# Windowed attention and a two-layer network on one core: a new written order of all steps, first-layer sums in any order of head pairs, copies on other engines, more DMA transposes, no warming matmuls

## The chip, the core and the metric

The kernel runs on one core of a Trainium2 chip. The metric is the device time of one execution in microseconds (us). A profiled execution has a span too, from its first to its last instruction; the span is what the views of the profile divide up, and it is a little shorter than the time.

## The reference

Eight batches of eight heads of width 64 attend; each batch has 512 local and 32 global tokens. What comes out, 544 tokens a batch and 512 wide, goes through two dense layers with a hard swish between them.

```python
k_all = concatenate([k_g, k_l]);  v_all = concatenate([v_g, v_l])
out_g = softmax(q_g @ k_all.T / 8) @ v_all                 # 32 global queries see all 544 keys
s_ll  = where(abs(i - j) <= 32, q_l @ k_l.T / 8, -1e9)     # 512 local queries: a band of local keys
s_lg  = q_l @ k_g.T / 8                                    # ... and the 32 global keys
out_l = softmax(concatenate([s_lg, s_ll])) @ concatenate([v_g, v_l])
x     = concatenate([out_g, out_l])                        # as (8 * 544, 512): heads side by side
h     = x @ w_in                                           # 512 -> 2048
out   = (h * clip(h + 3, 0, 6) / 6) @ w_out                # 2048 -> 512
```

Inputs and output are float32; the kernel multiplies in float16 and sums in float32.

## The kernel before

**Units of work.** The attention part goes by head pair: pair p (0 to 31) is two heads of batch p // 4, put side by side so that they fill the 128 partitions. The dense part goes by batch f (0 to 7) for the local tokens and once more (f = 8) for the 256 global tokens of all batches. The first layer makes 16 blocks c of 128 hidden rows by 512 tokens, each a sum of four matmuls, one for each head pair m of the batch (`w_in` is kept as four tiles by m). The second layer makes four quarters t of 128 tokens by 512 outputs, each a sum of sixteen matmuls over c.

**A list of tokens.** Nothing is in a loop. The whole program is one list of words, `ORDER` (L514 on), 2069 of them, which `run(ORDER.split())` (L688) takes one after the other; each word names a small helper and its arguments. `pin(*ALL)` (L689) then ties the instructions of every engine, and those of the SP queue that starts the transfers, into the order in which they were written. So an engine does its instructions in the order of the list, and each waits where its operands or its output buffer are not ready. A second string, `SEATS`, gives for each tile in turn the number of the buffer that it takes: seven PSUM banks `ps0` to `ps6` (the eighth holds the global output), 13 staging buffers for loads, three or four for most others.

**The words**, by helper (an engine letter at the end of a word is v for VectorE, g for GpSimd, a for ScalarE):

- `ld`, `lw`, `lg`, `lv`: load one pair's q, k or v (256 KB of float32 to a staging tile), a piece of the weights, the global q and k, the global v. All but `lv` (GpSimd's queue) go by the SP queue.
- `ca`, `cw`, `Gc`: cast what was loaded to float16 (`copy`, L133). `vs`, `vg`, `vG`, `kg`, `qw`: shift or copy pieces of v, of the global v and k, and the wrap of 32 columns of q. `fv`, `fg`, `fe`, `fk`, `ov`, `qz`, `iv`, `ig`, `im`, `ik`: fills of constants and masks.
- `Tp` and `Te`: transpose q or k on TensorE (four 128-wide matmuls) and copy it out of PSUM; or `Td` (L243): the same by a DMA transpose, one instruction of the SP queue. `Gp`, `Ge` do it for the global q and k.
- `Sp` (L286): scores of a pair for one of two windows of keys (ch 0 and 1), eight matmuls over 64 rows into two banks. `Se` (L296): exponential of one bank on ScalarE. `Sv` (L300): product with the 0/1 mask on VectorE. Where `Sm` ran first (two 512-wide matmuls adding -30000 outside the band), there is no `Sv`.
- `Ap` (L333, L336) and `An` (L345, L346): attention times values, and division by the sum of the exponentials, on VectorE. `Qp`, `Qe`, `Pp`, `Ga`, `Gv`: the same for the global queries.
- `Xp` and `Xe`, or `Xd` (L372): transpose the normalised result into the activations `xt` of the dense part, on TensorE with a copy, or by a DMA transpose.
- `Hp` (L408): matmuls m0 to m1 of first-layer block c of batch f. `Ha` (L413): relu of (h + 3) / 6 on ScalarE. `Hv` (L419): min with 1 and times h on VectorE, which frees the PSUM bank. `Op` (L426): four of the sixteen matmuls of a quarter t. `Oe`: copy it out. `Os` (L442): store it.
- `wm` (L495): warming matmuls, 512 wide on zeros, whose result nothing reads.

**How the order is staged.** The list opens with batch 0's loads, casts and scores, with the weights' loads among them; from then on the dense part of batch f is written between the attention steps of batch f + 1, and the loads for later batches with them. The last stretch has only dense work. The two lines that fix the order of a first-layer sum before are in `H_pe`: the bank is taken when `m0 == 0`, and the sum starts at m == 0 and stops at m == 3; so pair 0 is first and pair 3 last. `O_pe` is written in the same way over c.

The functions that the diff touches:

Of the kernel before, what the change touches and what calls it, by code (L numbers as in the profile page):

```python
# [14 lines left out]
def kernel(  # L15
# [40 lines left out]
ps 01234560123455401054036254631405623160243524341624132540134236503651631653106451034561204513240513015320465  # L56
10465461530421350623061350464301354063406342630456230452543025362350652436056504132653640306431463142301645341
20463213256016243056410263425130130512215321504260621365031640351202635410345265436513246164024325251206130541
52651341056201456104352614306241356525041236012453561031204215463245632456016061346521340264035640256010623416
5 ;  # L60
stg 0123456789abc0145362798b0a1c53647289a0b1c356489a27b103c645892a7b103c6589247bac03592681ba47053268cb17403529
a61cb748309c6b75831a65b4a3c ;
kn 01320132013201320132031013210323 ;
qn 01230123012301203132132302130213 ;
qT 01230213021302130203210230130202 ;
E 01210210210212012010210210201021 ;
xn 01201201201202102101201210210210 ;
t1 01230120120320321032103210321032103210321032103120312013023102310231213201320132013213023120312031201231023
1030132103123012312121302130213013012 ;
ot 0123023230120230301101303132132013  # L70
# [327 lines left out]
    gts = {}  # L398

# [3 lines left out]
    def H_pe(f, c, m0, m1):  # L403
        if m0 == 0:
            st["H", f, c] = ps_tile("psH")
        for m in range(m0, m1):
            x = xg[:, m].rearrange("p b s -> p (b s)") if f == B else xts[f, m]
            nc.tensor.matmul(out=st["H", f, c][:, 0:FN(f)], lhsT=w_in_t[m][:, c * P:(c + 1) * P],  # L408
                             rhs=x, start=(m == 0), stop=(m == NM - 1), skip_group_check=True)
# [12 lines left out]
    def O_pe(f, t, c4):  # L422
        if c4 == 0:
            st["O", f, t] = ps_tile("po")
        for c in range(4 * c4, 4 * c4 + 4):
            nc.tensor.matmul(out=st["O", f, t][:, 0:dm], lhsT=gts[f, c][:, t * P:(t + 1) * P],  # L426
                             rhs=w_out_t[c // 4][:, c % 4], start=(c == 0), stop=(c == NC - 1))
# [87 lines left out]
id ld.1.q iv wm.7 ld.1.k fg.1.v ld.0.q fv.0.v ld.2.q lg.k.0 fv.1.v ld.0.k ca.1.q.g ld.3.k lv.0 Tp.1.q ov.1.0  # L515
ld.2.k ca.1.k.g Te.1.q.a ld.3.q ig ov.0.0 Tp.1.k qw.1.v ld.0.v ov.0.1 lw.i.7 im Gc.k.0.g ov.0.2 ld.1.v
Te.1.k.v Gp.k.0 ov.0.3 ca.0.k.g lw.i.4 Ge.k.0.v ca.2.q.g lw.i.12 Tp.0.k Te.0.k.v lw.i.0 Tp.2.q Sm.1.0 Te.2.q.a
ca.3.k.v Sm.0.0 vg.0.2.v ca.0.q.a vg.0.1.v Sm.1.1 ca.2.k.g lw.i.3 kg.0.v Tp.0.q vg.0.0.v fk.0 Te.0.q.a Sp.1.1
ld.2.v Sp.1.0 Se.1.1.1 qw.0.v Sp.0.0 Se.1.0.1 Sp.0.1 ca.0.v.g ld.3.v Se.0.0.0 wm.4 vs.0.g ca.3.q.a lw.i.1
Se.0.1.0 qw.2.g Tp.3.k Tp.2.k Se.0.1.1 Sm.2.0 Te.2.k.v ca.1.v.g lw.i.5 Se.1.1.0 ik vs.1.g Se.1.0.0 Sp.2.0  # L520
lw.i.2 Sm.2.1 Se.0.0.1 vg.0.3.g Sv.0.1.0 lw.i.8 Sv.0.1.1 Sp.2.1 Se.2.0.0 cw.i.12.g Tp.3.q cw.i.7.v Se.2.0.1
Ap.0.1 lw.i.6 cw.i.0.g Te.3.q.v Ap.0.0 Se.2.1.1 Ap.1.0 lw.i.13 cw.i.4.g qw.3.v Te.3.k.a Ap.1.1 An.1.0 Sm.3.0
Se.2.1.0 An.0.0 Sm.3.1 ca.2.v.g lw.i.10 fe.0 An.1.1 Sp.3.0 vs.2.g Sp.3.1 An.0.1 Se.3.0.0 Xp.1 ca.3.v.g lw.i.9
Se.3.0.1 Xp.0 Ap.2.0 Xe.0.v vs.3.g Ap.2.1 Se.3.1.1 lw.o.0 An.2.0 Hp.0.7.0.1 Se.3.1.0 cw.i.1.g Hp.0.1.0.1
lw.i.11 An.2.1 Hp.0.3.0.1 Xe.1.a Ap.3.1 Ap.3.0 cw.i.3.a cw.i.2.g ld.4.q An.3.1 Hp.0.1.1.2 Xp.2 qz Hp.0.5.0.1
cw.i.5.v lw.i.14 Hp.0.3.1.2 An.3.0 Hp.0.2.0.2 cw.i.6.g lw.o.1 Hp.0.7.1.2 Xe.2.a Xp.3 Hp.0.5.1.2 ov.1.1 Xe.3.v
Hp.0.2.2.3 Hp.0.7.2.3 fe.1 fe.3 cw.i.8.v lw.i.15 Hp.0.7.3.4 Hp.0.1.2.4 Ha.0.7 lw.o.7 Hp.0.10.0.1 Hp.0.4.0.1
Ha.0.1 Hp.0.4.1.2 Hv.0.7 Hp.0.5.2.3 cw.i.9.g lw.o.2 Hp.0.4.2.3 ov.1.2 Hp.0.4.3.4 Hv.0.1 cw.i.10.g Hp.0.2.3.4
ld.4.k cw.i.13.a Hp.0.5.3.4 Hp.0.0.0.1 cw.o.0.g Hp.0.0.1.2 Ha.0.2 lg.k.1 Hp.0.0.2.3 cw.i.11.g Hp.0.0.3.4
Ha.0.5 Hp.0.3.2.3 Hv.0.2 Hp.0.11.0.2 Ha.0.4 Hp.0.11.2.3 fe.2 Hp.0.10.1.2 cw.i.14.g Hp.0.10.2.3 Ha.0.0 Hv.0.4  # L530
Hp.0.10.3.4 Hp.0.11.3.4 ca.4.q.g Hp.0.9.0.1 Ha.0.10 lw.o.3 Hv.0.0 Hp.0.9.1.3 cw.o.1.g ov.1.3 Hp.0.9.3.4
cw.i.15.v lg.q.0 Tp.4.q Hp.0.14.0.1 Ha.0.9 Hv.0.10 Hp.0.14.1.3 Ha.0.11 Hp.0.14.3.4 Hv.0.9 Hp.0.12.0.2
Hp.0.3.3.4 Hv.0.5 Hp.0.12.2.4 Ha.0.3 ca.4.k.g Hp.0.13.0.1 Te.4.q.v Hp.0.13.1.2 Ha.0.14 Hp.0.13.2.3 lw.o.5
Hv.0.3 Hp.0.13.3.4 Hp.0.6.0.1 Ha.0.12 Gc.k.1.g lw.o.6 Hp.0.6.1.2 Hv.0.14 Hp.0.6.2.3 Ha.0.13 lw.o.4 Gp.k.1
cw.o.3.g Hv.0.12 Hp.0.6.3.4 Hp.0.8.0.1 ld.5.q cw.o.2.g Hp.0.8.1.2 Ha.0.6 Ge.k.1.v Hp.0.8.2.3 Hv.0.13
Hp.0.8.3.4 ld.5.k Hp.0.15.0.1 Tp.4.k lw.o.8 kg.1.v Op.0.1.0 Te.4.k.a fk.1 cw.o.7.v lw.o.11 Ha.0.8 Hv.0.11
cw.o.5.g Op.0.2.0 lw.o.10 qw.4.v Hv.0.6 cw.o.6.g lw.o.9 Sp.4.1 Gc.q.0.g lw.o.13 Hv.0.8 Hp.0.15.1.2 Se.4.1.0
Hp.0.15.2.4 lw.o.12 Se.4.1.1 Gp.q.0 Op.0.0.0 ca.5.q.g lw.o.15 cw.o.4.a Sv.4.1.1 Ha.0.15 Ge.q.0.v Op.0.0.1
lw.o.14 Hv.0.15 cw.o.8.g ld.6.q Sp.4.0 ca.5.k.g Qp.0 cw.o.11.v ld.4.v Se.4.0.1 Qp.3 Op.0.1.1 Sv.4.1.0 lv.1
Se.4.0.0 ld.6.k Qe.3 Tp.5.k fg.0.g Sv.4.0.0 Qp.1 ld.5.v Op.0.2.1 cw.o.10.v cw.o.9.a Te.5.k.a ld.7.q Op.0.1.2  # L540
vG.0.g Qe.0 cw.o.12.v ld.8.k cw.o.13.g Tp.5.q Qe.1 Sv.4.0.1 Op.0.0.2 ld.7.k cw.o.15.g Te.5.q.a Pp.0 cw.o.14.v
ld.6.v Pp.1 qw.5.v Op.0.0.3 ca.6.q.v ld.7.v Tp.6.q Op.0.1.3 Oe.0.0.a ca.4.v.g ld.8.q Te.6.q.a Sp.5.1 Oe.0.1.a
vs.4.v Sp.5.0 vg.1.0.g vg.1.3.v Op.0.2.2 Se.5.1.0 vg.1.2.v vg.1.1.v qw.6.g Se.5.0.0 ca.6.k.v ld.10.q Ap.4.1
Se.5.0.1 Ap.4.0 Tp.6.k Se.5.1.1 Op.0.2.3 An.4.0 ca.5.v.g ld.9.q Te.6.k.a An.4.1 Qp.2 Sv.5.1.0 ld.9.k Sp.6.0
Qe.2 Sp.6.1 vs.5.v Oe.0.2.v Op.0.3.0 Se.6.0.0 ca.7.q.v Se.6.1.0 ld.11.v Xp.4 Sv.5.0.0 Tp.7.q Se.6.1.1 Qp.6
Sv.6.1.0 Qp.4 ca.7.k.g Xe.4.a Op.0.3.1 Sv.6.1.1 Se.6.0.1 Sv.5.1.1 Op.0.3.2 Sv.5.0.1 Te.7.q.a Sv.6.0.1 Qe.4
# [135 lines left out]
Hp.8.13.1.3 Op.8.1.0 Op.8.1.1 Hp.8.8.3.4 Op.7.2.3 Ha.8.8 Hv.8.8 Hp.8.13.3.4 Hp.8.12.3.4 Op.7.3.1 Oe.7.2.a  # L682
Ha.8.13 Os.7.2 Op.8.1.2 Ha.8.12 Hv.8.13 Hv.8.12 Op.7.3.2 Op.8.1.3 Op.7.3.3 Oe.8.1.v Op.8.0.0 Os.8.1 Oe.7.3.a
Oe.7.1.a Op.8.0.1 Op.7.0.0 Os.7.3 Op.8.0.2 Os.7.1 Op.8.0.3 Op.7.0.1 Oe.8.0.a Op.7.0.2 Os.8.0 Op.7.0.3 Oe.7.0.a
Os.7.0
"""

    run(ORDER.split())  # L688
# [31 lines left out]
```

## Time and profile before

| what | value |
|---|---|
| runs of the kernel | 322.07, 318.54, 321.63 us (median 321.63) |
| span of the profiled execution | 318.3 us, 7431 instructions |
| mean granted TensorE clock | 0.991 |
| TensorE busy | 306.1 us (96%), 2787 matmuls |
| VectorE busy | 222.1 us (70%), 538 instructions |
| ScalarE busy | 217.6 us (68%), 434 |
| GpSimd busy | 86.8 us (27%), 155 |
| DMA | 53.06 MB, mean 167 GB/s |

The engines run side by side, so the shares don't add up to one. Matmuls are pipelined, and their busy time says that one was in the array, not how densely they follow each other; the spacing of their starts says that. Busy GpSimd lies in the first half above all (five to seven tenths of each of the first six slices of a fortieth of the span, nothing in the last nine). The profiled execution's own time is its span and what lies around it; the runs in the table are timed without the profiler, and the span is 0.2 us below the lowest of them.

### The profile page before, as it was taken

The numbers are of one execution on the slowest core, as the hardware profiler recorded it, in microseconds if no ns is written. First come the engines' busy times: TensorE is split into PE (matmuls) and PEld (weight loads), VectorE is DVE, ScalarE is ACT, GpSimd is POOL, SyncE is SP. The second block draws the span as 40 slices with busy tenths as digits, with TensorE's granted clock in tenths as the row PEclk, the third lists the DMA queues.
The fourth block names the chain that finished last, engine by engine and source line by source line (L and its number), as shares of the span: only waits on it lengthen the run. The fifth ranks groups of instructions, "written<-read, shape, count | busy, mean of one in ns | idle before, by whom it ended". The sixth has DMA issues, their size and how long they took to land.

```text
span 318.3 us, 7431 instructions
## 1 busy us (share of the span) xinstructions
PE 306.1 (96%) x2787; PEld 161.6 (51%) x2787; DVE 222.1 (70%) x538; ACT 217.6 (68%) x434; POOL 86.8 (27%) x155
## 2 busy tenths in 40 slices
PE   5889999999999999999998999999999999999994
PEld 1554455754555554554553546445555546456541
DVE  6496986979998996688753885589638667486120
ACT  5589787889656866878666986586748853477031
POOL 5766574723310223151103812412003000000000
PEclk9799999999999999999999999999999999999998
DMA  7999999598899988999999995694541004400033
GB/s 220 300 260 365 249 355 268 113 178 170 201 173 215 234 185 176 206 190 184 193 237 202 242 224 105 140 208 94 142 107 59 2 16 101 148 3 0 0 97 104
DMA packets 140293, 53.06 MB, mean 167 GB/s; under 512 B 127712, under 2 KB 131808, under 8 KB 140256
## 3 DMA queue, kind: packets, MB, share of 16 engines
q1 hardware_dynamic: 138080, 52.32, 71.8%
q0 software_dynamic: 2176, 0.26, 1.3%
q8 instruction: 22, 0.36, 0.5%
q14 instruction: 15, 0.12, 0.1%
HBM read 35.13 MB, written 8.91 MB: 138 GB/s over the span
## 4 chain that ended last, share of the span: by engine, by line
PE 84%; DVE 8%; DMA 3%; ACT 1%; issue 1%; SPq 1%; POOL 1%; DVEq 0%
PE psH L408 35%; PE po L426 34%; PE psS L286 5%; PE pav L333 2%; PE pav L336 2%; DVE E L300 2%; PE pg L360 2%; DMA xt<-xn 2%; DMA stg<-in_k_g_dram 1%; DVE xn L346 1%; PE psSG L310 1%; ACT E L296 1%; PE psS L274 1%; DVE gt L419 1%; PE psTq L248 1%
## 5 line engine op out<-in xcount | busy, mean ns | idle before, releaser
L426 PE MATMUL po<-wout,gt 128*128 128x512 f16 x544 | 131.7, 379 | 0.1
L408 PE MATMUL psH<-xt,win 128*128 128x512 f16 x512 | 125.2, 379 | 1.4 <-DMA xt<-xn 1.2
L419 DVE SCALAR_TENSOR_TENSOR gt<-t,psH 128x512 f16<-128x512 f32 (+1 forms) x144 | 89.0, 652 | 37.3 <-ACT t L413 36.2
L413 ACT ACTIVATE t<-psH,half_col 128x512 f32<-128x512 f32 (+1 forms) x144 | 89.6, 666 | 32.7 <-PE psH L408 27.7
L296 ACT ACTIVATE E<-psS 128x512 f16<-128x512 f32 x128 | 68.9, 609 | 26.0 <-PE psS L286 22.0
L408 PEld LDWEIGHTS <-win 128*128 128x128 f16 x576 | 53.0, 98 | 53.3 <-issue 1.8
L426 PEld LDWEIGHTS <-gt 128*128 128x128 f16 x544 | 49.2, 97 | 50.5 <-issue 0.4
L300 DVE TENSOR_TENSOR E<-E,mk 128x512 f16<-128x512 f16 x112 | 49.2, 469 | 15.3 <-ACT E L296 14.9
L346 DVE TENSOR_TENSOR xn<-pav,rc 128x256 f16<-128x256 f32 x64 | 27.2, 424 | 2.2
L133 ACT COPY ot<-po 128x512 f32<-128x512 f32 x23 | 13.3, 589 | 21.7 <-PE po L426 18.4
L333 PE MATMUL pav<-vt,E 128*128 128x65 f16 x256 | 22.9, 193 | 0.6 <-DVE qT L133 0.3
L336 PE MATMUL pav<-vb,E 128*128 128x65 f16 x256 | 22.9, 193 | 0.2
L333 PEld LDWEIGHTS <-E 128*128 128x128 f16 x256 | 18.9, 97 | 5.0 <-DVE E L300 0.5
L286 PEld LDWEIGHTS <-kT 64*128 64x128 f16 x512 | 14.6, 94 | 13.3 <-issue 11.1
L286 PE MATMUL psS<-qT,kT 64*128 64x128 f16 x512 | 21.0, 217 | 0.3 <-DVE qT L133 0.3
L345 DVE RECIPROCAL rc<-pav 128x4 f32<-128x4 f32 x64 | 11.2, 175 | 13.3 <-PE pav L336 13.1
L336 PEld LDWEIGHTS <-E 128*128 128x128 f16 x256 | 17.6, 97 | 4.8 <-issue 0.4
L133 POOL CAST qn<-stg 128x512 f16<-128x512 f32 x20 | 13.0, 651 | 24.7 <-DMA stg<-in_q_l_dram 24.4
L133 POOL CAST vt<-stg 128x512 f16<-128x512 f32 x20 | 12.9, 643 | 24.9 <-DMA stg<-in_v_l_dram 20.1
L133 POOL COPY vb<-vt 64x512 f16<-64x512 f16 x20 | 12.7, 640 | 23.0 <-DVE vt L133 17.6
L133 POOL CAST kn<-stg 128x512 f16<-128x512 f32 x15 | 10.4, 694 | 27.5 <-DMA stg<-in_k_l_dram 25.1
L314 ACT ACTIVATE Eg<-psSG 128x256 f16<-128x256 f32 x32 | 12.6, 392 | 5.3 <-PE psSG L310 3.3
(89 smaller groups left out, 248.3 us busy)
## 6 DMA issues: line engine op xcount, KB each, us to landing
stg<-in_q_l_dram SPq DMA_DIRECT2D x32, 256.0 KB, 4.0
stg<-in_k_l_dram SPq DMA_DIRECT2D x32, 256.0 KB, 3.9
stg<-in_v_l_dram SPq DMA_DIRECT2D x32, 256.0 KB, 3.9
out_dram<-ot SPq DMA_DIRECT2D x24, 256.0 KB, 3.2
stg<-in_moe_w_in_dram SPq DMA_DIRECT2D x16, 256.0 KB, 5.8
stg<-in_moe_w_out_dram SPq DMA_DIRECT2D x16, 256.0 KB, 5.1
out_dram<-ot SPq DMA_DIRECT2D x8, 192.0 KB, 2.7
out_dram<-ot SPq DMA_DIRECT2D x16, 64.0 KB, 1.9
```

The lines of the kernel that those rows point to most:

```text
L133: (nc.scalar.copy if eng == "a" else ENG[eng].tensor_copy)(out=out, in_=in_)
L286: nc.tensor.matmul(out=st[p, ch][e][:, w * P:(w + 1) * P], lhsT=kT[r, c0:c0 + P], rhs=qT[r, w * P:(w + 1) * P], start=not added, stop=True ...
L296: nc.scalar.activation(out=E_of(p)[:, ch, e], in_=st[p, ch][e], func=EXP, scale=qk_scale)
L300: nc.vector.tensor_tensor(out=E[:, ch, e], in0=E[:, ch, e], in1=mk[:, ch].rearrange("p w c -> p (w c)"), op=mult)
L314: nc.scalar.activation(out=Eg[:, 0:NT].rearrange("p u e s -> p (u e s)"), in_=ps[:, 0:NT * 2 * Sg], func=EXP, scale=qk_scale)
L333: nc.tensor.matmul(out=o, lhsT=E[:, 0, e, w * P:(w + 1) * P], rhs=vt[:, w, h, 0:D + 1], start=True, stop=False, skip_group_check=True)
L336: nc.tensor.matmul(out=o, lhsT=E[:, 1, e, w * P:(w + 1) * P], rhs=vb[:, (w - 1) % NT, h, 0:D + 1], start=False, stop=True, skip_group_chec ...
L346: nc.vector.tensor_tensor(out=st[p, "xn"][:, 2 * w2:2 * w2 + 2].rearrange("p w (e d) -> p w e d", e=2), in0=pv[:, :, :, 0:D], in1=rc.to_br ...
L408: nc.tensor.matmul(out=st["H", f, c][:, 0:FN(f)], lhsT=w_in_t[m][:, c * P:(c + 1) * P], rhs=x, start=(m == 0), stop=(m == NM - 1), skip_gr ...
L413: nc.scalar.activation(out=t1[:, 0:FN(f)], in_=st["H", f, c][:, 0:FN(f)], func=RELU, bias=half_col, scale=1.0 / 6.0)
L419: nc.vector.scalar_tensor_tensor(out=gts[f, c][:, 0:n], in0=st["t", f, c][:, 0:n], scalar=1.0, in1=st["H", f, c][:, 0:n], op0=amin, op1=mult)
L426: nc.tensor.matmul(out=st["O", f, t][:, 0:dm], lhsT=gts[f, c][:, t * P:(t + 1) * P], rhs=w_out_t[c // 4][:, c % 4], start=(c == 0), stop=( ...
```

## The change

`ORDER` and `SEATS` are replaced as a whole (2162 words for 2069), and two helpers are changed so that the terms of a sum may be written in any order:

```diff
+    added = {}
...
     def H_pe(f, c, m0, m1):
-        if m0 == 0:
+        if ("H", f, c) not in st:
             st["H", f, c] = ps_tile("psH")
         for m in range(m0, m1):
+            k = added["H", f, c] = added.get(("H", f, c), 0) + 1
             x = xg[:, m].rearrange("p b s -> p (b s)") if f == B else xts[f, m]
             nc.tensor.matmul(out=st["H", f, c][:, 0:FN(f)], lhsT=w_in_t[m][:, c * P:(c + 1) * P],
-                             rhs=x, start=(m == 0), stop=(m == NM - 1), skip_group_check=True)
+                             rhs=x, start=(k == 1), stop=(k == NM), skip_group_check=True)
...
     def O_pe(f, t, c4):
-        if c4 == 0:
+        if ("O", f, t) not in st:
             st["O", f, t] = ps_tile("po")
         for c in range(4 * c4, 4 * c4 + 4):
+            k = added["O", f, t] = added.get(("O", f, t), 0) + 1
             nc.tensor.matmul(out=st["O", f, t][:, 0:dm], lhsT=gts[f, c][:, t * P:(t + 1) * P],
-                             rhs=w_out_t[c // 4][:, c % 4], start=(c == 0), stop=(c == NC - 1))
+                             rhs=w_out_t[c // 4][:, c % 4], start=(k == 1), stop=(k == NC))
...
     ORDER = """
-id ld.1.q iv wm.7 ld.1.k fg.1.v ld.0.q fv.0.v ld.2.q lg.k.0 fv.1.v ld.0.k ca.1.q.g ld.3.k lv.0 Tp.1.q ov.1.0
-ld.2.k ca.1.k.g Te.1.q.a ld.3.q ig ov.0.0 Tp.1.k qw.1.v ld.0.v ov.0.1 lw.i.7 im Gc.k.0.g ov.0.2 ld.1.v
...
+fk.0 lg.k.0 lv.0 iv ov.0.0 ov.0.1 ov.1.0 ld.3.k id ig Gc.k.0.g fv.1.v ov.0.2 qz ov.1.1 im ld.1.k fv.0.v vg.0.1.v
+ov.0.3 ca.1.k.a ld.1.q ld.3.q ca.1.q.a ca.3.q.v Sm.1.1 ca.3.k.v Gp.k.0 Ge.k.0.v Tp.1.q Te.1.q.a qw.1.v Tp.1.k Tp.3.q
...
```

What the new list holds, word against word:

| words | before | after |
|---|---|---|
| `wm` (warming) | 2 words, 11 matmuls | none |
| `Sm` / `Sv` (mask by matmul / by product) | 8 / 112 | 7 / 114 |
| `Td`, `Xd` (DMA transposes of k and of activations) | 22, 23 | 24, 25 |
| `Tp` of k, `Xp` (the same on TensorE) | 10, 9 | 8, 7 |
| `ca` of k, q, v on GpSimd | 15, 20, 20 | 4, 3, 8 |
| ... on VectorE | 9, 8, 8 | 19, 21, 8 |
| ... on ScalarE | 8, 4, 4 | 9, 8, 16 |
| `vs` on GpSimd / VectorE / ScalarE | 20 / 12 / 0 | 4 / 15 / 13 |
| `vg` on GpSimd / VectorE / ScalarE | 12 / 16 / 4 | 9 / 18 / 5 |
| `qw` on GpSimd / VectorE | 18 / 14 | 5 / 27 |
| `Oe` (copy out of the second layer) on ScalarE / VectorE | 23 / 11 | 15 / 19 |
| `Hp` | 478 words, 576 matmuls | 576 words, 576 matmuls |

The `Hp` words now name one matmul each, and a block may begin with any pair. The first loads on the SP queue are those of k_g, then k of pairs 3 and 1 and q of pairs 1 and 3; before they were q and k of pair 1, q of 0 and 2, then k_g. Apart from the mask words, what is computed from what is the same.

## The prediction

> **What bounds the kernel now.** I read the page first (engine shares, clock, chain of waits), then the windows and the chain of the first 27 us, then the groups by line and shape for prices.
>
> ```profile
> PE 306.1 (96%) x2787; PEld 161.6 (51%) x2787; DVE 222.1 (70%) x538; ACT 217.6 (68%) x434; POOL 86.8 (27%) x155
> PEclk9799999999999999999999999999999999999998
> PE 84%; DVE 8%; DMA 3%; ACT 1%; issue 1%; SPq 1%; POOL 1%; DVEq 0%
> ```
>
> TensorE is busy 96% of the span, and the chain that ended last runs through it for 84%. A busy share hides how densely matmuls follow each other, so I price TensorE by spacing, from the chain and the timeline: 52 output matmuls take 11.24 us (0.216 each); a 256-wide one 0.109, a 128-wide transpose 0.056, an attention-value one 0.0295, a global score 0.029, a global value 0.025, a block of eight score matmuls 0.27.
>
> ```profile
> 2.79 4.47 DMA stg<-in_k_g_dram
> 7.31 0.60 POOL kgn L133
> ...
> 13.26 1.00 ACT E L296 x2
> ...
> 302.79 11.24 PE po L426 x52
> 314.03 0.02 issue
> 314.05 0.59 ACT ot L133
> ```
>
> Before in these prices: 1083 512-wide (512 first layer, 544 second, 16 masks, 11 warming) 233.6, 64 256-wide 7.0, 512 attention-value 15.1, 116 transposes 6.5, 64 score blocks 17.4, 320 global values 8.0, 160 global scores 4.6, global transposes 1.0: 293.2 us. The span is 318.3, so 25.1 us are not matmul work. Set against the written order, the timeline says where: the first matmul of first-layer block 10 of batch 0 starts at 27.30, with 15.6 us of work written ahead of it: 11.7 us are lost by then. From there to the last matmul 8.9 more are lost; 4.5 lie between the last matmul's issue and the end (its drain, the copy at 314.05, the store). Of the 8.9, some 4 are changeovers to and from the 64-row score matmuls (in the timeline 0.312 instead of 0.216 into a block, 0.148 instead of 0.03 out of it, 35 runs of blocks, part of it in the block's price); 1.4 is one stall at 168.4 on a transposed activation.
>
> **The change, part by part.** *Removed TensorE work.* Eleven warming matmuls (2.4 us by spacing), one mask token of two (0.4), four transpose tokens of four (0.9): 3.7 us less, 289.5. The order comparison agrees: 58 fewer rows, 29 matmuls with their weight loads. All else on TensorE is only reordered; taking head pairs in any order costs nothing by itself, as start and stop follow the count.
>
> *The start.* Before, the chain waits for the fifth load, k_g, landing at 7.26; its cast, two casts queued behind it on GpSimd and the masks bring the first exponential to 13.16. After, k_g is the first load; by the first landing before (issue 0.75, landing 3.40) it is in by about 3. Then ACT sets the pace: table load to 2.02, six fills of ones at 0.51 to 0.61 and the 1.1 us zeroing to about 6.8, two casts to 8.0, the first query copy to 9.4 (waiting for four cold transposes), the key copy to 10.0. The first exponential comes near 10.7. Twenty more ACT instructions follow (fifteen exponentials, three copies out of transposes, a cast, a shift) at their queued spacing of 0.5, to 21.3; two half copies of q_g to 22.2. So the first-layer matmuls begin near 20 and are fed from about 23.5, when 12.0 us of work are written ahead: lag 11.5. I add 0.5 for the half-speed clock (below): 12.0 against 11.7, +0.3. The other start costs (casts of w_in on GpSimd at 0.63, last load landing near 27 by the 0.65 spacing of landings) stay ahead of the matmuls that need them by 2 us or more. Bounds: 10.0 if everything starts 2 us sooner, 14.5 if GpSimd's queue (a wrap copy that waits for ACT's tenth instruction, five casts behind it) is late.
>
> The warming matmuls ran at half clock, and what they bought was lost again before the masks:
>
> ```profile
> 5.33:8.75 3.42, 0.89 (x11) 0.62 (x12) 1.88 (x9) 2.12 (x5) 2.21 (x7) 1.00 1.10 287
> 8.75:12.16 3.41, 3.25 (x15) 1.42 (x14) 2.84 (x7) 1.10 (x2) 2.25 (x4) 0.54 1.16 331
> ```
>
> Columns: window; length; busy and count of PE, PEld, DVE, ACT, POOL; granted clock; DMA share; GB/s. The clock is full only while 0.89 us of matmuls run and 0.54 while the masks do. Without warming the sparse matmuls from 4 to 13 us run cold, about 3 us of work at double cost; ACT's queue covers most, since 0.5 us per exponential exceeds the cold price of half a score block. Uncovered: 3 us. The Trainium skill ("TensorE: Matmul & The Clock Gate", Part 1) says that the array starts at half rate, is released by a busy window of some 3.4 us and falls back after an idle one. It speaks against removing warming; by it alone the loss is at most half a window, an estimate of 1.7 us. The trace agrees on the fallback (row above).
>
> *Copies on other engines.* GpSimd gives up 40 casts (x 0.66), 13 wraps (0.30), 16 shifts (0.64) and 9 others (0.62): 46 us. VectorE takes 23 casts (0.42 to 0.47), 13 wraps (0.17 to 0.37), 8 output copies (0.69), two mask products, three shifts: +20. ScalarE takes 17 casts (0.62), 13 shifts (0.61), 8 others (0.6) and sheds 8 output copies (0.59) and 5 more: +15.
>
> ```profile
> L133 POOL CAST qn<-stg 128x512 f16<-128x512 f32 x20 | 13.0, 651 | 24.7 <-DMA stg<-in_q_l_dram 24.4
> L133 DVE CAST wout<-stg 128x512 f16<-128x512 f32 x5 | 4.0, 807 | 0.0
> L133 ACT CAST kn<-stg 128x512 f16<-128x512 f32 x8 | 4.8, 613 | 0.0
> L133 DVE CAST qn<-stg 128x512 f16<-128x512 f32 x8 | 3.7, 469 | 0.0
> L300 DVE TENSOR_TENSOR E<-E,mk x112: 404/418/867, 17.3 to 267.5; 128x512 f16<-128x512 f16 x112
> ```
>
> The last line (min/median/max ns) has a mean of 469: where GpSimd is idle (after 245 us) the product takes 437, and the same cast 418 to 905. An emptier GpSimd should so return some 6 us of products and 4 of casts. The cover is TensorE; most of it lies here:
>
> ```profile
> 60.00:190.00 130.00, 128.44 (x1263) 67.81 (x1256) 103.73 (x249) 99.42 (x202) 38.30 (x70) 1.00 0.98 195
> ```
>
> ```profile
> 75.00:100.00 25.00, 25.00 (x284) 13.85 (x283) 23.43 (x60) 16.93 (x35) 6.72 (x13) 1.00 0.90 178
> ```
>
> The changed order leaves GpSimd about 1 of the 38 there; VectorE goes to about 115 of 130 and ScalarE to 113, 88%, from 80 and 76. VectorE already ran at 94% from 75 to 100 us with TensorE busy throughout (last row), so I charge only +0.4: 9.3 lost later. Bounds: -3.4 (the changeovers and 1.5 us of waits remain) to +13.6 (ScalarE's waits of 30.6 us in the stretch all stay and its added 13.6 come on top); nearer the low end, because ScalarE's waits are mostly for work not yet due.
>
> *DMA.* Four more DMA transposes: 71 for 67, at 1.2 us of the SP queue each, 4.9 us, in a queue that issues back to back from 62 to 195. They replace four on TensorE and four PSUM copies of 0.6. Counting SP's issue times, the tightest transposes of the second and third batch have 13 to 14 us of lead against 18 to 21 before; an activation lands 2.7 us after issue. Taken as hidden; 1.4 us a time if not.
>
> *Tail.* The last three stores follow each other by 0.9 us instead of 2.5, but the last is one DMA instead of two: 0.
>
> Sum: -3.7 + 0.3 + 0.4 = **-3.0 us**, a span of 315.3. The profiled span lies 3.3 under the median of 321.63 and 0.2 under the lowest run; I carry the same distance: **318.6**. One per cent (3.2 us) is about what a measurement of this kernel can tell from no change.
>
> **Rivals.** *Better fed (313):* the later lag falls by 3.4, the stalls on VectorE and the activation gone because GpSimd no longer slows VectorE: 318.6 - 3.4 = 315.2; with the start at its lower bound (-2.0) 313.2. For it: the product's 867 against 418. Against: TensorE waited only some 5 us in the whole middle.
>
> *Nothing gained (321.5):* the clock stays cold through the start (+2.0 of the 3), three waits of 0.3 us on global scores written only 0.6 to 1.5 us of matmuls ahead of their use add 0.9: the 3.0 are gone. For it: the chain begins at the start; against: ACT, not TensorE, paces it.
>
> *Slower, full queues (326):* in the 130 us stretch ScalarE waits 30.6 us now. With 113 us of work 17 are left. Where its waits are for results that come when they come, they stay: with all of them it would be 13.6 late, with three quarters (23) 6, and it decides from the point where more than 17 stay. The middle of 0 and 13.6 gives 318.6 + 7 = 325.6. Behind a late copy on ScalarE stands a first-layer activation, behind that the product which frees the PSUM bank, and then TensorE. For it: 30 of its 38 added instructions are casts and shifts that wait for a load. Against: the 94% row of VectorE.
>
> *Slower, late transposes (324):* each of four batches waits 1.4 us, as once before: +5.6.
>
> **Chances.** Forecast 0.34, better fed 0.27, nothing gained 0.15, full queues 0.15, late transposes 0.09. The forecast lies at the 1% line and is split: 0.17 faster, 0.14 same, 0.03 slower. So faster 0.17 + 0.27 = 0.44, same 0.14 + 0.15 = 0.29, slower 0.03 + 0.15 + 0.09 = 0.27. Range 311.5 to 326; the forecast's own is 315 to 321.
>
> **What would show it.** Start right: first exponential near 10.7, 512-wide first-layer matmuls dense by 24, k_g off the chain. Clock: one stretch at 0.5 ending before 17; a second one while first-layer matmuls run would be wrong. Copies right: mask product mean near 0.42, POOL under 45 us, VectorE near 235, ScalarE near 232, TensorE's waits after 27 us about 9. Wrong if PSUM-bank waits on the first-layer activation or waits on transposed activations sum to over 4 us, or the median lies outside the range.

## The result and the profile after

| | before | after |
|---|---|---|
| median of the runs | 321.13 us (318.54 to 322.07) | 334.45 us (334.28 to 336.68) |
| ratio | | 1.044, 95% interval 1.0386 to 1.0493 |
| profiled execution: its time, span | span 318.3 | 334.28, span 332.5 |

One run of e7 below, 337.35 us, fell in a slow state of the chip and is left out of its numbers. The change made the kernel 13.3 us slower; the forecast was 318.6 us, 3.0 faster, in a range of 311.5 to 326. The page of after, its shares, clock and summary of the chain:

```profile
PE 305.5 (92%) x2758; PEld 160.8 (48%) x2758; DVE 234.6 (71%) x588; ACT 233.7 (70%) x460; POOL 42.8 (13%) x77
PEclk9999997999999999999999999999999999999999
PE 49%; DVE 18%; DMA 16%; ACT 6%; issue 4%; SPq 3%; POOL 2%; POOLq 0%; DVEq 0%; ACTq 0%
```

The busy sums came out as forecast. The third line is the finding: TensorE's share of the chain fell from 84% to 49%, and DMA rose from 3% to 16%, VectorE from 8% to 18%. VectorE and ScalarE are far from full, and yet TensorE is no longer nearly all that the end waits for. The chain itself (start, length, work; some of its longer pieces, in order of time):

```profile
3.98 3.86 issue
...
24.18 6.48 DMA stg<-in_moe_w_in_dram
...
36.75 5.44 DMA stg<-in_q_l_dram
42.89 8.17 DMA vg<-in_v_g_dram
51.38 4.48 DVE E L299 x6
...
86.05 4.71 DMA qT<-qn
...
127.62 3.85 DMA stg<-in_k_l_dram
...
316.71 12.10 PE po L428 x56
```

k_g's load is off the chain, as forecast. In its place stand loads of `w_in`, of q, of the global v and of k and transposes of q; before's chain had only k_g and one transposed activation as its longer transfers.

**Where the 14.2 us of span lie.** As in the prediction I price TensorE's instructions by spacing and take, for the instruction that has P us of such work written ahead of it, its start less P. That lag, in us:

```
P =              12     30     50     60     90    120    250    end
before         11.6   11.9   13.5   13.6   14.9   16.2   20.6   25.0
after          12.9   13.7   20.7   21.0   25.2   32.5   39.1   43.0
```

The lag grew by 18.0 and the work fell by 3.7. Of the 18.0, 1.3 are in the start, 5.5 between P = 30 and 50 (44 to 71 us in after), 3.0 between 50 and 90, 6.0 between 90 and 120 (about 115 to 152 us), 2.2 from there to 250, 0.5 between 12 and 30; the tail gave back 0.5. The prediction's "later lag" (12 to 250) is 9.0 before and 26.2 after. Single stops of TensorE of more than 0.18 us after 24 us sum to 3.4 us before and to some 20 after. The waits (engine, line, releaser, us in all, times, longest), from 27 us on, the five largest of after and the largest of before:

```profile
PE psH L409 <- DVE gt L420: 2.5, 4, 1.4
PE pav L332 <- DVE E L299: 2.5, 2, 2.2
PE psH L409 <- DMA xt<-xn: 2.2, 2, 1.5
PE psS L285 <- DVE ot L132: 2.2, 1, 2.2
PE pav L335 <- DVE vb L132: 1.4, 2, 1.1
```

```profile
PE psH L408 <- DMA xt<-xn: 1.2, 1, 1.2
```

Most of these waits are for VectorE, each behind something different: a product, a piece of v, an output copy, a first-layer product. The stretches (window; length; busy and count of PE, PEld, DVE, ACT, POOL; granted clock; DMA share; GB/s), of after:

```profile
5.33:8.75 3.42, 1.97 (x18) 1.58 (x18) 1.86 (x10) 2.72 (x6) 0.83 (x2) 1.00 1.00 280
50.00:62.00 12.00, 7.97 (x67) 4.05 (x67) 10.77 (x19) 4.35 (x9) 10.33 (x16) 0.86 0.60 120
60.00:190.00 130.00, 120.76 (x1185) 64.09 (x1186) 103.74 (x276) 101.14 (x202) 3.77 (x6) 1.00 1.03 192
75.00:100.00 25.00, 24.00 (x240) 12.75 (x239) 20.28 (x54) 22.50 (x46) 0.00 (x0) 1.00 1.12 198
```

and of before, the one that the prediction didn't look at:

```profile
50.00:62.00 12.00, 11.70 (x184) 7.81 (x183) 10.29 (x30) 10.63 (x25) 6.54 (x12) 1.00 0.84 194
```

From 50 to 62 us TensorE does 67 instructions instead of 184. VectorE is busy as long as before for 19 instructions instead of 30: they became longer. GpSimd, which gave up half of its work over the run, has *more* of it here (10.33 for 6.54). What VectorE does there (start, length, idle time before in brackets):

```profile
51.08 0.28 DVE L132 COPY vb<-vg 32x512 f16<-32x512 f16 x1 [1.46 <-DMA vg<-in_v_g_dram]
51.38 4.48 DVE L299 TENSOR_TENSOR E<-E,mk 128x512 f16<-128x512 f16 x6
55.78 0.83 DVE L132 CAST wout<-stg 128x512 f16<-128x512 f32 x1
56.53 2.77 DVE L299 TENSOR_TENSOR E<-E,mk 128x512 f16<-128x512 f16 x2
```

It waits 1.46 us for the global v (issued by GpSimd), then takes 4.48 us for six mask products whose median is 0.42, and 2.77 for the next two. GpSimd beside it:

```profile
57.02 0.57 POOL L172 DMA_DIRECT2D vg<-in_v_g_dram  x1
```

The first of those two products (0.8 us) lies beside GpSimd's casts, the second (57.27 to 59.30, 2.03 us) beside two issues of global v, of which this is one, and the cast and copy between them. And in the written order of after three products of pairs 5 and 6 stand ahead of pair 4's last one, for which TensorE waits: it ends at 54.36, and attention times values of pair 4 starts at 54.42 after a stop of 2.37. The tile view (min/median/max ns) of the product against 404/418/867 before:

```profile
L299 DVE TENSOR_TENSOR E<-E,mk x114: 410/421/2031, 17.9 to 279.6; 128x512 f16<-128x512 f16 x114
```

The SP queue is held up at the same time (its own timeline, after):

```profile
53.14 0.89 SPq L147 DMA_DIRECT2D stg<-in_v_l_dram  x1
60.76 3.22 SPq L371 DMA_TRANSPOSE xt<-xn  x2
64.03 0.57 SPq L147 DMA_DIRECT2D stg<-in_k_l_dram  x1
...
72.43 1.59 SPq L242 DMA_TRANSPOSE kT<-kn  x1
```

Before, the same transpose of k of pair 8 stands here:

```profile
62.49 1.30 SPq L243 DMA_TRANSPOSE kT<-kn  x1
```

From 54.0 to 60.8 the queue starts nothing: the transpose of the activations of pair 4 is at its head and waits for VectorE, which is late for the reason above. Six loads of batch 2 are written behind it. So the queue is through with the transpose of k of pair 8 at 74.0 instead of 63.8, ten us late (the ends of these rows; the data land 2.3 and 3.1 us later). From there it issues almost back to back to 199.6 us, in before from 62.5 to 192.1 (211.5 and 208.4 us of issue in all), and it hardly catches up: the transpose of k of pair 24, near the end of that stretch, starts at 196.4 instead of 187.9. What is late next are casts of loads, on engines that now do them in order between other work:

```profile
131.49 0.43 DVE L132 CAST kn<-stg 128x512 f16<-128x512 f32 x1 [2.67 <-DMA stg<-in_k_l_dram]
```

VectorE idles 2.67 us for a load; five places behind that cast stands the copy that frees the PSUM bank for which TensorE stands from 131.49 to 133.70.

### The profile page after: what moved, and what is told of

It reads as the page before. It is cut to its first block, busy times and chain, and to the rows that moved or that the text cites. A ratio compares the mean times of both kernels' runs of the same rounds, so it can differ in the third digit from the quotient of the medians.

```text
span 332.5 us, 7330 instructions
## 1 busy us (share of the span) xinstructions
PE 305.5 (92%) x2758; PEld 160.8 (48%) x2758; DVE 234.6 (71%) x588; ACT 233.7 (70%) x460; POOL 42.8 (13%) x77
## 4 chain that ended last, share of the span: by engine, by line
PE 49%; DVE 18%; DMA 16%; ACT 6%; issue 4%; SPq 3%; POOL 2%; POOLq 0%; DVEq 0%; ACTq 0%
PE po L428 24%; PE psH L409 17%; DVE gt L420 7%; DVE E L299 4%; DMA stg<-in_moe_w_in_dram 3%; PE psS L285 3%; DMA stg<-in_q_l_dram 3%; DMA qT<-qn 3%; DMA vg<-in_v_g_dram 2%; DMA stg<-in_k_l_dram 2%; ACT t L414 2%; ACT E L295 2%; PE pav L335 1%; PE pav L332 1%; DVE vb L132 1%
## 5 line engine op out<-in xcount | busy, mean ns | idle before, releaser
L409 PE MATMUL psH<-xt,win 128*128 128x512 f16 x512 | 126.5, 379 | 5.9 <-DVE gt L420 2.5
L295 ACT ACTIVATE E<-psS 128x512 f16<-128x512 f32 x128 | 67.9, 607 | 17.6 <-PE psS L285 17.2
L285 PE MATMUL psS<-qT,kT 64*128 64x128 f16 x512 | 22.1, 220 | 4.5 <-DVE ot L132 2.2
L132 DVE COPY ot<-po 128x512 f32<-128x512 f32 x19 | 13.1, 688 | 15.9 <-PE po L428 12.8
L132 ACT COPY ot<-po 128x512 f32<-128x512 f32 x15 | 8.9, 590 | 20.7 <-PE po L428 19.9
L132 POOL CAST qn<-stg 128x512 f16<-128x512 f32 x3 | 1.8, 612 | 157.8 <-ACT t L414 157.0
L359 PEld LDWEIGHTS <-vt 128*128 128x128 f16 x256 | 10.9, 96 | 5.0 <-DVE xg L394 0.4
L132 DVE CAST qn<-stg 128x512 f16<-128x512 f32 x21 | 8.8, 431 | 5.0 <-DMA stg<-in_q_l_dram 5.0
```

Of the source, the lines that this page charges most:

```text
L132: (nc.scalar.copy if eng == "a" else ENG[eng].tensor_copy)(out=out, in_=in_)
L285: nc.tensor.matmul(out=st[p, ch][e][:, w * P:(w + 1) * P], lhsT=kT[r, c0:c0 + P], rhs=qT[r, w * P:(w + 1) * P], start=not added, stop=True ...
L295: nc.scalar.activation(out=E_of(p)[:, ch, e], in_=st[p, ch][e], func=EXP, scale=qk_scale)
```

## The experiments

Before's own median lies between 319.93 and 321.50 us on the chips of these runs, so kernels are compared by their ratio to before on the same chip. After's ratio is 1.044. A table of lags stands at the end.

**Engines alone, order alone.** e1 takes after's order and seats with before's engine for every copy that both have; e2 the reverse.

```diff
# e1, against after (195 words, in 155 places)
-ca.1.k.a ... Te.1.k.a ... vs.1.v ... cw.i.7.g
+ca.1.k.g ... Te.1.k.v ... vs.1.g ... cw.i.7.v
# e2, against before (195 words, in 177 places)
-ca.1.q.g ca.1.k.g ... Te.1.k.v ... vs.1.g
+ca.1.q.a ca.1.k.a ... Te.1.k.a ... vs.1.v
```

> The changed order and seats, but every cast, shift, wrap and copy that both lists have goes back to the engine it had before (GpSimd again for 46 us of it). Theory 'engines': the lost 17 us after the first 27 us come from copies that wait for a load or a global value in VectorE's and ScalarE's in-order queues, with the products that free PSUM banks behind them (2.5 us each for the casts of the global q at 116.5, of k of pair 18 at 131.5, of q of pair 26 at 217.6). Back on GpSimd such a wait holds up nothing, so the time falls by 8 to 14 us, to 320 to 326, and VectorE's waits for loads (now 12 us) go to under 3. Theory 'order': loads and DMA transposes are late on the SP queue whoever casts; the time stays at 331 to 336.

> The order and seats of before, with the engines of the changed kernel for every copy that both have. Theory 'engines': the copies bring their waits with them to VectorE and ScalarE, 328 to 335. Theory 'order': the loads come as early as before, so the copies find them there; 319 to 323. If both act together (the new order alone is harmless and the new engines alone are), this is near 321 and the other mixture too.

e1: 344.68 us, 1.0722 (1.0668 to 1.0775). e2: 338.78, 1.0563 (1.0474 to 1.0653). Both theories fall. The order (with its buffers) alone costs 23.3 us, the engines alone 17.4; if they added, after would be 40.7 slower, and it is 13.3. So the loss can't be shared out between the two; the likeliest reading is that each list is an order and an assignment that fit each other. They also lose elsewhere (table below): e1 has 9 us more lag than after by P = 30 already, e2 takes on 12.2 from 120 to 250.

**The wait for global v.** e3 moves one load in GpSimd's queue.

```diff
-... ca.6.k.v ca.6.q.g Tp.6.q lv.1 Te.6.q.v
+... Ap.3.0 Gc.q.0.g lv.1 vs.0.a     # and none there
```

> The changed kernel with one load moved: the global v of batch 1 is issued on GpSimd's queue near 18 us instead of 42.9. In the changed kernel it lands near 51; VectorE waits 1.46 us for it, GpSimd 3.8, and then GpSimd's piled-up copies run beside VectorE's mask products, which take 0.82 us each instead of 0.42. Theory 'a late load piles copies up': the stretch from 50 to 61 us loses 1 to 2 us instead of 5.7, so the time falls by 3 to 5, to 329.5 to 331.5. Theory 'the stretch is too full for VectorE anyway': at most the wait of 1.5 goes, 333 to 334.5.

335.64, 1.0426 (1.0363 to 1.0489): nothing gained. The wait of 1.46 is gone, but the next loads of global v slid beside the product that TensorE waits for (54.22 to 55.99, 1.77 us), and the stop there grew from 2.37 to 3.30.

**Warming alone.** e4 is before without its two `wm` words.

```diff
-id ld.1.q iv wm.7 ld.1.k
+id ld.1.q iv ld.1.k          # and wm.4 likewise
```

> The kernel before without its eleven warming matmuls, nothing else changed. As predicted, the removed work of 2.4 us by spacing is set against up to 3 us of cold matmuls in the start that ScalarE's queue mostly covers: minus 2 to 0, 319.5 to 321.5. Rival: the warming matmuls lie in a time when TensorE waits for loads and nothing is gained at all, and the cold masks and scores make the first exponential later: plus 1 to plus 2, 322 to 323.5.

320.36 against 321.37, 0.997 (0.9939 to 1.0002): the warming matmuls bought nothing that can be measured, and leaving them out is no cause of the loss.

**Waits that hold up what is queued behind.** e5 gives nine copies that wait for a load or a transpose to GpSimd, which is nearly empty by then.

```diff
-qw.11.v qw.13.v ca.17.q.v ca.18.k.v ca.18.q.v Gc.q.4.v ...
+qw.11.g qw.13.g ca.17.q.g ca.18.k.g ca.18.q.g Gc.q.4.g ...
```

> The changed kernel, order and seats as they are; nine copies that stood idle in VectorE's queue (one in ScalarE's) for a transfer, 0.7 to 2.7 us each and 13.2 us in all, go to GpSimd, which has nothing from 66 to 220 us: the casts of the global q (of batches 4 to 7), of k and q of pair 18, q of 17 and 26, k of 11 and 25, and the wraps of 11 and 13. Theory 'waits in order': these waits are what stopped TensorE at 117.5, 133.7, 106 and 216 (1.5, 2.4, 1.1, 0.9 and what follows each); 5 to 9 us less than the changed kernel, 326 to 330. Theory 'late transfers': the SP queue is late, the next copy waits for the next load instead; 0 to 2 less, 332.5 to 334.5.

336.47, 1.0466 (1.043 to 1.0501): no gain. The waits moved to transposed activations (2.2 us in after), here from 62 us on:

```profile
PE psH L409 <- DMA xt<-xn: 4.0, 4, 1.5
```

Here it is the transfer that is late; where the wait for it stands made no difference to the time.

**The SP queue relieved.** e6 leaves out the stores of four batches.

```diff
-Os.0.0 Os.0.3 Os.1.1 Os.0.2 ... Os.3.2 Os.3.3
```

> The changed kernel without the sixteen stores of batches 0 to 3 (twenty transfers), which hold the SP queue for some 12 of its 126 back-to-back microseconds from 74 to 200; those output rows are left unwritten. Theory 'late transfers': every load and DMA transpose behind them comes earlier, by up to 12 us at 200, and the stalls on them (at 106, 117, 133, 148, 216) shrink to nothing: 7 to 10 us less than the changed kernel, 324 to 328. Theory 'waits in order, or a queue that is full on VectorE': little is given back, 331 to 334.

329.44, 1.0241 (1.0198 to 1.0284), the lowest ratio of all edits of after: 5.0 us by the medians, 6.4 by the ratios. The lag from P = 90 to 120 grows by 3.4 instead of 7.3. The edit takes away the queue's issues and the transfers as well; e16 below keeps the transfers, and there this stretch grows by 2.9, which speaks for the queue's issues as what bounds it.

**Fewer copies on GpSimd beside the products.** e7 gives eight of them to VectorE and writes three loads of global v earlier.

```diff
-vg.1.0.g cw.o.4.g ca.4.v.g vs.4.g vg.1.3.g cw.o.7.g vg.1.2.g ca.7.k.g
+vg.1.0.v cw.o.4.v ca.4.v.v vs.4.v vg.1.3.v cw.o.7.v vg.1.2.v ca.7.k.v   # lv.1 lv.2 lv.3 earlier
```

> The changed kernel with eight copies of the stretch from 47 to 58 us taken from GpSimd and given to VectorE (about 2.9 us more work there), and the loads of the global v of batches 1 to 3 issued near 37 to 40 us. Theory 'shared access': beside GpSimd's copies a mask product takes 0.82 instead of 0.42, and 1.8 to 2.0 where GpSimd writes a transfer's descriptors; without them VectorE is through earlier although it does more, the stall of 2.4 us at 54 and the 3 after it shrink to 1 to 2 in all: 3 to 4.5 less than the changed kernel, 330 to 331.5. Theory 'VectorE has too much to do there': the stall grows by 2 to 3, 336.5 to 337.5.

332.30, 1.0349 (1.0307 to 1.0391): some 2 to 3 us less than after, at the edge of the noise. The twelve products of pairs 4 to 6 keep VectorE busy for 8.9 us in after, 4.8 in before, 5.4 here. But with the copies taken over, VectorE's work from 27 us to pair 6's second division is still 31.8 us, for 32.8 in after and 28.4 in before: the slow products are real, and curing them this way mostly changes what fills VectorE.

**The free order of the sums.** e8 puts the first-layer words of a block together again.

```diff
-Hp.0.6.0.1 Hp.0.5.2.3 Qe.3 Hp.0.7.2.3
+Hp.0.5.0.1 Hp.0.5.2.3 Hp.0.6.0.1 Hp.0.7.2.3 Qe.3    # and so on, 244 places
```

> The changed kernel, in which inside each unbroken run of first-layer matmuls the same matmuls are written block by block as far as their operands and banks allow (430 of 576 change place, every block still ends in time for its activation; from the first to the last matmul of a block lie 5.8 first-layer matmuls on average instead of 10.8, and 7.2 before). Theory 'free order costs nothing': within 1 us of the changed kernel, 333.5 to 335.5. Theory 'many open blocks': they end in a burst, so ScalarE and VectorE start late and then block the banks; block by block is 2 to 5 faster, 329.5 to 332.5. Theory 'free order is useful': the blocks now wait for the last transposed pair, slower, 336 to 339.

335.83, 1.0446 (1.0426 to 1.0466): the same as after. The free order of the pairs is no cause of the loss.

**The head of the SP queue.** e9 puts the two waiting transposes back on TensorE; e10 writes six loads ahead of them; e11 puts the fault into before: four loads behind a waiting transpose.

```diff
# e9
-Xd.4 ... Xd.5
+Xp.4 Xe.4.a ... Xp.5 Xe.5.v
# e10
-ld.6.v ld.10.q ld.8.q ld.7.v lv.2
+ld.6.v ld.10.q ld.8.q ld.7.v ld.8.k ld.8.v ld.9.q ld.9.v ld.9.k ld.10.k lv.2
# e11, against before
+Td.8.k ld.10.q ld.9.q ld.9.k ld.11.v     # and none at their earlier places
```

> The changed kernel, in which two of the DMA transposes that the change added (the activations of pairs 4 and 5) are done as before, by four matmuls and a copy each. In the changed kernel they head the SP queue at 54.0 us and wait until 60.8 for the late normalisation of pair 4, and the six loads behind them (k and v of 8, q and v of 9, k of 9 and 10) start at 64.0 to 71.8. Theory 'a waiting transpose holds up the loads': the queue goes on at 54, those loads come 7 to 12 us earlier, the back-to-back stretch starts so much earlier and its stalls after 75 us (some 11 us) shrink by half or more: 5 to 9 less than the changed kernel, 325.5 to 329.5. Theory 'the queue is full anyway': only its own 2.5 us are saved, 331.5 to 333.

> The changed kernel with those six loads written ahead of the two DMA transposes, and nothing else moved; the queue has the same work. Theory 'a waiting transpose holds up the loads': as in the run before, 326 to 330, or a little above, since the transposes stay. Theory 'the queue is full anyway': 333 to 335. Rival that spoils both: the loads come earlier and find their staging buffers taken, so the queue waits there for a cast: 334 to 336.

> The kernel before, with the same fault put in: four loads (q of 10, q and k of 9, v of 11) that it issues from 53.3 to 57.0 are written behind the DMA transpose of k of pair 8, which waits until 62.5. Theory 'a waiting transpose holds up the loads': they come 9 us later, the stretch behind them is 3.7 us late, and TensorE loses 2 to 6: 323.5 to 327.5. Theory 'the queue's order is not what matters': within 1 us of the kernel before.

e9: 335.19, 1.0466 (1.04 to 1.0531). e10: 333.08, 1.0379 (1.0329 to 1.0429). e11: 324.02 against 321.50, 1.0092 (1.0047 to 1.0137). The injected fault costs 2.5 us, but taking it out of after gives at most 1.4 by the medians (2.0 by the ratios), and the intervals overlap. In e10 k of pair 8 has landed early, but its cast on VectorE ends only at 70.7, and its transpose at 71.9 instead of 74.0. In e9 the queue does go on at 54.2, with four of the loads, and then stands at the next transpose, that of q of pair 10:

```profile
57.36 1.06 SPq L147 DMA_DIRECT2D stg<-in_v_l_dram  x1
71.78 1.29 SPq L242 DMA_TRANSPOSE qT<-qn  x1
```

It waits for a cast that ScalarE does only at 71.12, behind steps of pair 7 for which it had stood idle. So another late operand took the place at the head, and the queue won nothing.

**Two and three causes together.** e12 is e10 with e7. e14 gives twelve casts of batch 2 to GpSimd; e13 is e10 with e14. e16 starts the stores of four batches from GpSimd's queue; e17 is e13 with e16.

```diff
# e14 (twelve casts)
-ca.8.q.v ca.10.q.a ca.8.k.v ca.8.v.a ... ca.10.v.a
+ca.8.q.g ca.10.q.g ca.8.k.g ca.8.v.g ... ca.10.v.g
# e16
-            nc.sync.dma_start(out=out[at:at + nr, :], in_=st["ot", f, t][r0:r0 + nr, :])
+            (nc.gpsimd if eng == "g" else nc.sync).dma_start(out=out[at:at + nr, :],
+                                                              in_=st["ot", f, t][r0:r0 + nr, :])
```

> The two edits together on the changed kernel: six loads ahead of the two waiting transposes, and from 47 to 58 us eight copies from GpSimd to VectorE with the global v loaded near 37 to 40 us. If the stall at 54 to 61 and the late queue are two causes, their gains add: 1.5 to 2 more than the loads alone, 324.5 to 328. If the stall is late only because of the loads or the loads only because of the stall, no more than the better of the two.

> The changed kernel with the six loads ahead of the two waiting transposes, and all twelve casts of pairs 8 to 11 on GpSimd, which is idle from 62 us. Theory 'the cast stands behind dense work': k of pair 8 is cast by 62, its DMA transpose ends near 67 instead of 71.9, the whole back-to-back stretch of the SP queue moves up by 5 to 7 us, and TensorE's stalls after 75 us shrink by as much: 325 to 328.5. Rival 'VectorE and ScalarE set the stretch': transposes earlier, the stalls the same, 331 to 333.5.

> The changed kernel with only the twelve casts of pairs 8 to 11 on GpSimd; the loads still start at 64 to 72 us behind the waiting transposes. Theory 'each holds the other': the first transpose ends near 70 to 71 instead of 74.0; 1 to 3 less than the changed kernel, 331 to 333.5. Theory 'casts alone': 326 to 329. Theory 'VectorE and ScalarE set the stretch': 333.5 to 335.

> The changed kernel with the sixteen stores of batches 0 to 3 started by GpSimd instead of the SP queue. Theory 'the SP queue is the bound of the stretch from 74 to 200': as when these stores were left out, 4 to 6 less, 328.5 to 330.5. Theory 'moved cost': writing their descriptors on GpSimd holds up VectorE's mask products (1.8 to 2.0 us where the global v's loads did so), the gain is lost: 332 to 336. The transfers share the DMA engines with the loads as before, so a gain would be the queue's, not the traffic's.

> All three together. If the late start of the queue's stretch and its length are what TensorE waits for after 75 us, the gains add: 320 to 325, some 10 to 13 under the changed kernel, with the stretch from 50 to 62 us (some 5 us of stalls) still there. If VectorE and ScalarE set the stretch, 329 to 333.

e12: 333.66, 1.0387 (1.0341 to 1.0433), no faster than e10. e14: 333.87, 1.0427 (1.0394 to 1.046). e13: 331.41, 1.0354 (1.0289 to 1.0418). e16: 333.44, 1.0411 (1.0345 to 1.0477). e17: 330.36, 1.0334 (1.0284 to 1.0384). In e13 the transpose comes early, on the SP timeline:

```profile
61.77 3.18 SPq L371 DMA_TRANSPOSE xt<-xn  x2
...
66.35 1.22 SPq L242 DMA_TRANSPOSE kT<-kn  x1
```

It ends at 67.6, which is 6.4 of the 10.2 us; the loads alone gave 2.1 and the casts alone 1.4 (72.6): each was hidden behind the other. At the end of the back-to-back stretch 4.6 of the 6.4 are left (k of pair 24 at 191.8 instead of 196.4). The time moved by 3.0, by the medians; the intervals of e13 and after still overlap a little. e16 shows the same on another resource: the growth of the lag from 90 to 120 falls to 2.9 from 7.3, and between 50 and 90 it rises to 6.9 from 4.5, for there VectorE now waits 3.1 us for a transposed q. Stores left out gave 5.0; stores moved to another queue, 1.0.

**Order of the products.** e18 is e13 with e7, and pair 4's products first on VectorE; e19 is e18 with e16.

```diff
-Sv.4.0.1 Sv.6.1.0 ... Sv.4.1.1 vg.1.1.v vg.1.3.g cw.o.7.g Sv.5.0.1 ld.7.k Sv.5.1.0 vg.1.2.g Sv.4.1.0 Sv.4.0.0
+Sv.4.0.1 Sv.4.1.1 ... Sv.4.1.0 Sv.4.0.0 vg.1.3.v cw.o.7.v cw.o.6.v ld.7.k vg.1.1.v vg.1.2.v Sv.5.0.1 Sv.5.1.0
```

> Loads ahead and casts of pairs 8 to 11 on GpSimd (331.4 measured), and in the stretch from 47 to 58 us eight copies from GpSimd to VectorE, with fourteen of VectorE's instructions there in the order in which TensorE uses them: the four products of pair 4 first (three of them stood behind products of pairs 5 and 6), then the copies that its values wait for, the casts of two pieces of w_out, the products of pair 5. Theory 'that stretch is a cause of its own': it loses 3 to 4.5 us instead of 7.6, the rest stays as it is, 327 to 328.5. Theory 'what is not lost there is lost later, on the SP queue or on ScalarE': 330 to 332.

> The same with the sixteen stores of batches 0 to 3 on GpSimd's queue. If the three causes add: 1 to 3 below the run before, 324 to 327. If the queue is no longer what TensorE waits for: as the run before.

e18: 330.33, 1.0288 (1.0228 to 1.0347). e19: 331.73, 1.033 (1.0279 to 1.0381). The stretch that lost most in after, in e18:

```profile
50.00:62.00 12.00, 9.38 (x94) 5.06 (x93) 11.36 (x32) 5.58 (x11) 5.76 (x10) 0.86 1.21 235
```

VectorE does 32 instructions there instead of 19, and TensorE no longer stops for pair 4. But it stops for pair 5 instead, at 55.47 for its products and at 57.42 for a piece of v:

```profile
PE pav L335 <- DVE vb L132: 1.7, 1, 1.7
PE pav L332 <- DVE E L299: 0.9, 1, 0.9
```

So from P = 30 to 50 the lag still grows by 5.9, for 7.1 in after, 7.8 in e13 and 1.6 in before: most of the stop was moved, not removed. No version beats before; e18 recovers 4.1 us of the 13.3 by the medians.

```
growth of lag   to 30  30-50  50-90  90-120  120-250   span
before           11.9    1.6    1.4     1.3      4.4  318.3
after            13.7    7.1    4.5     7.3      6.6  332.5
e1  order        22.9    7.3    3.1     7.4      7.5  342.6
e2  engines      14.3    2.3    5.5     3.8     12.2  335.9
e6  no stores    17.4    5.4    3.4     3.4      5.0  328.4
e13              14.2    7.8    1.1     5.1      6.3  327.9
e16              14.0    5.7    6.9     2.9      5.9  329.0
e18              13.9    5.9    1.1     6.8      7.5  328.5
```

Runs of one kernel spread by 2 to 4 us (e13: 329.65 to 333.51), so variants with ratios from 1.033 to 1.039 aren't told apart, and the spans are those of one execution.

## Why the prediction was wrong

**The step that failed is the later lag: "so I charge only +0.4".** It measured +17.2, above even its upper bound of 13.6. The step set the busy share of an engine in a stretch (88%) against a row in which VectorE had 94% and TensorE didn't wait. The busy times themselves came out near the forecast. The stretch of TensorE's work that before does from 60 to 190 us (P from 47 to 171) lies here in after:

```profile
67.60:206.80 139.20, 130.07 (x1240) 67.88 (x1239) 108.02 (x284) 113.08 (x223) 0.00 (x0) 1.00 1.02 189
```

ScalarE has 113.08 us in it (113 forecast) and VectorE 108.02 (115 forecast). Either would have fitted into 130 us, and yet the stretch took 139.2. So the amount of work isn't what binds, and concluding from it that TensorE would hardly wait had no ground. What grew are VectorE's waits for transfers in it: 0.2 us before, 9.2 in after, the two largest of them

```profile
DVE kn L132 <- DMA stg<-in_k_l_dram: 3.6, 2, 2.7
DVE qgn L132 <- DMA stg<-in_q_g_dram: 2.5, 1, 2.5
```

An engine that works through a fixed list waits at each late operand with all that stands behind it, and the row showed only that the *old* list had no such places. The step needed due times, not sums. The prediction did name the idle time of ScalarE and thought it harmless, "for work not yet due"; the two stops of TensorE that were followed back (at 54 and 133 us) have such idle time on VectorE behind them, and the SP queue stood for 6.7 us.

**"Taken as hidden; 1.4 us a time if not" failed in its form.** The lead of 13 to 14 us was counted in SP's issue times alone, as if the queue never stood. It stands 6.7 us at its head (54.0 to 60.8), and the lead is gone for everything behind it. The transposes of activations themselves cost little (2.2 us of waits against 1.2 before). What the step left out is that two of them stand ahead of six loads and wait there. That the queue's order costs time is shown by the fault in e11 (+2.5), and e6 and e16 speak for its issues as the bound from P = 90 to 120. No single part of it is the cause: e9 gives nothing and e10 1.4 us by the medians.

**"An emptier GpSimd should so return some 6 us of products" failed.** The sum of GpSimd fell (42.8 us, "under 45" was right) but 21.8 us of what is left lie between 27 and 66 us, where the slow products are. Mean 462 ns, not 420; the median is 421, so elsewhere it holds. The Trainium skill ("SBUF — State Buffer", Who interferes with whom) says that a VectorE instruction with two SBUF inputs contends with a GpSimd instruction that reads SBUF; the trace agrees, with 0.82 us instead of 0.42 beside a copy.

**The start, forecast +0.3, measured +1.3 by P = 12** and another 0.5 by 30. The first exponential came a little ahead of the 10.7 forecast:

```profile
10.13 0.60 ACT L295 ACTIVATE E<-psS 128x512 f16<-128x512 f32 x1 [1.17 <-PE psS L285]
```

The start went the way of the bound that I gave for a late GpSimd queue (its lag of 12.9 lies between the 12.0 forecast and that 14.5): the chain from 2 to 11.5 us has fills, k_g's cast, copies of the global k and v and a wrap on GpSimd.

**Right:** 3.7 us less TensorE work; the tail (0, measured -0.5); the free order of pairs at no cost (e8); warming worth nothing that can be measured (e4); VectorE 235 (234.6), ScalarE 232 (233.7). Signs of error that it set came: the median lies outside the range, and waits for the bank that a first-layer product frees (2.5) and for transposed activations (2.2) sum to 4.7, over 4. A second slow-clock stretch came too (the 7 in the clock row, 0.86 from 50 to 62 us), while second-layer matmuls ran: TensorE had stopped first (to 54.42), and of the four matmuls from 55.23 on most came some 0.4 us apart, which cost about 1 us more.

**The rivals.** "Full queues (326)" named the right side, and the work that it counted on arose: 113.08 us on ScalarE, whose idle time in the stretch is 26.1 us, more than the 17 of its condition. But TensorE's waits there are for VectorE and transposed activations, and 0.7 us of them for ScalarE; VectorE waits less for ScalarE's first-layer activations than before (6.6 us for 9.9). No run took the added work off ScalarE alone, so its share stays open. "Late transposes (324)" named the right queue and the wrong work in it. Together they had 0.24; neither alone would have reached 334.

**What stays open.** Three places are shown in the traces: VectorE's order and slow products from 50 to 62 us, the head of the SP queue with the casts behind it, the full SP queue after it. What each is worth in time is less sure. Leaving out the stores (e6, 5.0 us) is clear of the noise. Repairing the head of the queue (e13, 3.0) and the slow products (e7, about 2) is at its edge; e18 holds both repairs and keeps 9 us of loss, e19 is no faster with the stores moved. Which waits make up those 9 us, or whether they have a single cause, the runs don't tell. The factors of e1 and e2 rather say that order, engines and queue are one fit, in which each repair uncovers the next late thing, as e9 and e18 show in their traces. What the new `SEATS` cost by themselves wasn't tried: they stayed with their order in e1 and e2.

## What to carry to other kernels

When a kernel runs from fixed lists, an edit that moves copies or transfers can't be priced by busy sums, even where VectorE and ScalarE are busy 71% and 70%: for each moved instruction ask when its operand comes and what stands behind it, on each engine and on the queue that starts transfers, and look at the densest stretch by itself rather than at the mean. A queue that is back to back for 125 us carried 4.6 of 6.4 us at its head through to its end. If undoing each half of a change alone is worse than the whole (1.0722 and 1.0563 against 1.044), look for no single culprit.

## What the runs showed of the hardware that was not expected

- The granted-clock column can read 1.00 while matmuls come at half rate: in after the two 512-wide masks at 8.50 us start 0.43 us apart, and the windows of 5.33 to 8.75 and of 8.40 to 9.40 have 1.00; at 10.68 they are 0.216 apart. The trace has no clock record before 10.4 us, and the column reads full there. The spacing is the safer reading.
- The array can be slow again although work is at hand. In e6, from 20 to 27 us, far ahead of its edit:

```profile
20.00:27.00 7.00, 6.37 (x62) 4.10 (x59) 5.04 (x17) 4.37 (x8) 4.02 (x7) 0.51 0.84 249
```

  62 matmuls in 7 us where after has 111 at a clock of 1.00. It cost that execution some 3.7 us by P = 30 (17.4 against 13.7), so e6's profiled span understates what its edit gave.
- A mask product took 2.03 us beside GpSimd's issues of the global v loads, and the cast and copy between them, where beside a copy alone it took 0.82 and at the median 0.42. In e14, with one more cast between the two issues, it took 2.59. Which of them held it was not tried apart.
